# The first MLP product of the last token group by seven products of quarters, in matmuls of 128 columns

## The chip, the cores and the metric

The kernel runs on one core of a Trainium2 chip. A time is the device time of one execution in microseconds (us); lower is better. The kernel before takes 908.61 us, the median of three runs (908.17 to 909.64).

## The reference

Windowed causal attention over 8 batches, 8 heads, 576 positions and head size 64, with a linear bias, then an MLP on its output, all in float32:

```python
scores = scale * np.matmul(q, k.transpose(0, 1, 3, 2))
scores = np.where(mask, scores + bias[None], -1000000000.0)   # mask: 0 <= i - j < 128
attn = np.exp(scores - np.max(scores, axis=-1, keepdims=True))
attn = attn / (np.sum(attn, axis=-1, keepdims=True) + 1e-09)
x = np.matmul(attn, v).transpose(0, 2, 1, 3).reshape(B * S, H * D)     # 4608 x 512
h = x @ w_in                                                           # 512 x 2048
g = h * (1.0 / (1.0 + np.exp(-h)))
return g @ w_out                                                       # 2048 x 512
```

## The kernel before, in words

The 4608 tokens are worked in nine groups of 512 (group 0 to 8). A group's MLP has 16 steps, numbered through all groups (step 128 is the first of group 8, step 143 the last of all). A step makes one tile of 128 hidden features: its first product (`gemm1`) goes to a PSUM bank named `h`, of which there are two; `act1` (tanh, ScalarE), `act2` (multiply, VectorE), `act3` (the high half in f16, ScalarE) and `act4` (the low half, VectorE) make the activation; its second product (`gemm2`) adds into the banks of the output. Float32 precision comes from splitting every operand into a high and a low f16 half and multiplying three of the four pairs, so each product of 128 rows is three matmuls. The attention of the tokens to come is worked beside the MLP of the groups before.

Groups 7 and 8 (`FAST`) make the second product by Strassen's scheme in Winograd's form: seven products of quarters in place of eight, M1 to M7. For that a step is not one feature tile over 512 tokens, but two feature tiles (`j` and `j + 8`) over 256 tokens (`t` is 0 or 1): `gemm1_fast` fills one `h` bank with 2 x 12 matmuls of 256 columns, `act_sums` makes three sums of quarters of the activation, and `gemm2_fast` has 21 matmuls of 256 columns in two halves. The sums of `w_out` that the seven products need are made in advance by GpSimd (`SUM_WORK`), at positions 240 to 374, from late in group 3 to group 5. At the end of each eight steps `join_products` puts the output together from four banks.

The order of all work is written out by hand: a counter `pos` goes up by one for each half of a product, and `plan` holds for each position what else is issued there (`put`, `later`, `ahead`); each engine works its instructions in the order of issue. `LAG` says how many steps the second product stands behind the first in the last two groups: two before. `TAGS` constants name which finished buffer a new tile takes over.

Of the kernel before, what the change touches and what calls it, by code (L numbers as in the profile page):

```python
# [6 lines left out]
F32 = mybir.dt.float32  # L7
# [10 lines left out]
P = 128  # L18
# [12 lines left out]
TG = 512  # L31
# [36 lines left out]
Q16 = ("w1_2", "w1_3")  # L68
K16 = ("w1_4", "w1_5", "w1_6")
CUT = 2.0**-20  # L70
NB = 2
FAST = (NG - 2, NG - 1)
HALF_F = NF // 2
LAG = 2
SUMS, SUMS_STEP = 240, 18
OUT_TAGS = {3: ("w1_14", "w1_9"), 4: ("w1_13", "w1_14"), 6: ("w1_0", "w1_1")}
# [35 lines left out]
def tile_window_attention_then_silu_mlp(ctx, tc, qk, v, w_in, w_out, distance, out):  # L112
# [228 lines left out]
    def in_scale(b):  # L341

        if b == 0:
            wsc["in"] = pool.tile([P, NB], F32, tag="win", bufs=1, name="win")
            wsc["inv"] = pool.tile([P, NB], F32, tag="winv", bufs=1, name="winv")
            gsc["t", IN16] = pool.tile([P, NB], F32, tag="tsc", bufs=2, name=f"tsc{IN16}")
        n, inv = NF // NB, wsc["inv"][:, b : b + 1]
        scale_of(vred["w", 0]["m"][:, n * b : n * b + n], f"in{b}", 0, wsc["in"][:, b : b + 1], inv)
# [360 lines left out]
    def sum_lo(j, k):  # L709
# [4 lines left out]
        out16 = wsum[1, j]  # L714
        nc.gpsimd.tensor_sub(out16[:, 1], wsum["r"][:, 0, : DM // 2], out16[:, 0])

    def gemm1_fast(n, half):
# [53 lines left out]

    def act1(n):
        if n // NF in FAST:
            gact[n] = gt = pool.tile([P, 2 * TG], F32, tag="big", name=f"gt{n}")
# [64 lines left out]
    def gemm2_fast(n, half):  # L839
        g, (t, j) = n // NF, divmod(n % NF, HALF_F)  # L840
        last = LAST - 1 if n // HALF_F == LAST // HALF_F else n - j + HALF_F - 1
        if n == LAST:
            gemm2_last(half)
            return
        gh, gl, _ = gact.pop(n) if half else gact[n]
        products = (M5, M2, M1, M3) if half == 0 else (M4, M7, M6)
        for a, parts in ((gh, (0, 1)), (gl, (0,))):
            for k in products:
                b, side = PLACE[k]
                if j == 0 and side == 0 and a is gh:  # L850
                    ops[b] = psum.tile([P, DM], F32, tag=("axaz" if t else "wxyz")[b], bufs=2 if t and b % 2 == 0 else 1, name=f"m{g}_{t}_{b}")
# [52 lines left out]
    def join_products(g, t, half):  # L904

        scale = gsc[g][:, 2:3]
        if half == 0:
            st["out"] = [pool.tile([P, 2, DM // 2], F32, tag="q", bufs=2, name=f"of{g}_{t}_{k}") for k in range(2)]
# [229 lines left out]
    for j in range(HALF_F):  # L1138
        n = SUMS + SUMS_STEP * j
        for k, work in enumerate(SUM_WORK):  # L1140
            for fn, part in work:
                put(n + k, fn, j, part)
    put(STATS + 2 * NF + 6, out_scale)
    put(STATS + 2 * NF + 7, cut_scale)
    for which in range(2):
# [67 lines left out]
    with tc.manual_schedule():  # L1213
# [40 lines left out]
        for g in range(NG):  # L1254
# [3 lines left out]
            for f in range(NF):  # L1258
                n = g * NF + f
                waiting.append(n)  # L1260
                left = LAG if g in FAST else 1
                if f == NF - 1 and (g not in FAST or g == NG - 1):
                    left = 0
                seq += [("g1", n, 0), ("g1", n, 1)]
                while len(waiting) > left:
                    k = waiting.pop(0)
                    seq += [("g2", k, 0), ("g2", k, 1)]
            for k, n, half in seq:
                begin()
# [55 lines left out]
```

## Time and profile before

| what | value |
|---|---|
| runs of the kernel before | 908.17, 909.64, 908.61 us |
| the profiled execution's own time | 907.86 us |
| its span, first to last instruction | 905.7 us |
| TensorE matmuls busy | 896.4 us, 99% of the span |
| VectorE, ScalarE, GpSimd busy | 704.1, 584.0, 180.3 us |
| first products of groups 7 and 8 (L724) | 768 matmuls, 88.7 us |
| granted TensorE clock | 1.00 |

The page counts a matmul as busy until its modelled end, so the pace of TensorE is read from the starts of instructions in the timeline, not from their lengths. The last two groups run from about 743 us to the end; there the DMA engines and GpSimd have next to nothing to do.

### The profile page before, as it was taken

How to read it: one execution, taken by the hardware profiler on the slowest of the kernel's cores; microseconds unless marked ns; L12 is line 12 of the kernel's file. 1: busy time of each engine (PE TensorE's matmuls, PEld its weight loads, DVE VectorE, ACT ScalarE, POOL GpSimd, SP SyncE). 2: the span in 40 equal slices, each digit the busy share in tenths (PEclk: the TensorE clock that was granted, in tenths of full speed). 3: DMA queues.
4: the chain of work that ended last, by engine and by line, in shares of the span. 5: the costliest groups of instructions: out<-in, count | busy, mean ns of one | idle time of the engine just before them, and what ended most of it. 6: DMA issues, size and time to landing. Idle time of an engine off the chain costs nothing.

```text
span 905.7 us, 19202 instructions
## 1 busy us (share of the span) xinstructions
PE 896.4 (99%) x7369; PEld 591.5 (65%) x7369; DVE 704.1 (78%) x1755; ACT 584.0 (64%) x1200; POOL 180.3 (20%) x191
## 2 busy tenths in 40 slices
PE   9999999999999999999999999999999999999998
PEld 7877776888855555454445554455555558888887
DVE  6998998688978877677887787878776667667675
ACT  7789986776579855887666656657565554433342
POOL 2356662000000000012354332742000000000000
PEclk9999999999999999999999999999999999999999
DMA  9979724334489644994454536442753333000000
GB/s 323 398 180 268 233 58 129 71 94 94 105 218 232 179 94 120 241 229 120 88 147 106 106 80 144 99 99 59 158 123 95 69 77 77 12 13 24 1 25 24
DMA packets 198475, 113.58 MB, mean 125 GB/s; under 512 B 166256, under 2 KB 168432, under 8 KB 198384
## 3 DMA queue, kind: packets, MB, share of 16 engines
q1 hardware_dynamic: 197952, 111.97, 48.5%
q8 instruction: 58, 0.95, 0.5%
q10 hardware_dynamic: 432, 0.39, 0.1%
q14 instruction: 33, 0.27, 0.1%
HBM read 62.52 MB, written 9.44 MB: 79 GB/s over the span
## 4 chain that ended last, share of the span: by engine, by line
PE 84%; DVE 2%; ACT 1%; DMA 1%; issue 1%; DVEq 0%; ACTq 0%
PE o L946 29%; PE h L752 27%; PE h L724 9%; PE m L853 8%; PE av L582 4%; PE sp L477 3%; PE sp L484 2%; PE h L757 1%; DMA hl<-hr 1%; DVE gt L785 0%; DVE gl L829 0%; DVE v L458 0%; ACT wr L989 0%; ACT t L518 0%; ACT gh L815 0%
## 5 line engine op out<-in xcount | busy, mean ns | idle before, releaser
L946 PE MATMUL o<-w,gh 128*128 128x512 f16 (+1 forms) x896 | 273.6, 387 | 0.5 <-ACT gh L811 0.5
L752 PE MATMUL h<-xt,w 128*128 128x512 f16 (+1 forms) x1344 | 269.5, 349 | 0.0
L752 PEld LDWEIGHTS <-w 128*128 128x128 f16 x1344 | 126.4, 98 | 112.5 <-issue 3.3
L785 DVE SCALAR_TENSOR_TENSOR gt<-gt,h 128x512 f32<-128x512 f32 x144 | 98.5, 684 | 101.2 <-ACT gt L781 100.5
L781 ACT ACTIVATE gt<-h,tsc 128x512 f32<-128x512 f32 x128 | 87.4, 683 | 136.6 <-PE h L752 108.8
L946 PE MATMUL o<-w,gl 128*128 128x512 f16 (+1 forms) x448 | 172.1, 384 | 0.4 <-DVE gl L829 0.3
L518 ACT ACTIVATE t<-t,mx 128x256 f32<-128x256 f32 (+1 forms) x288 | 127.4, 488 | 42.8 <-DVE mx L508 41.4
L532 DVE SCALAR_TENSOR_TENSOR hr<-t,hr 128x512 f16<-128x512 f32 (+1 forms) x128 | 98.2, 772 | 16.8 <-ACT hr L527 16.2
L452 POOL TENSOR_SCALAR v<-rv,vsc 128x512 f16<-128x512 f32 x30 | 24.6, 820 | 419.6 <-DMA rv<-v 287.7
L946 PEld LDWEIGHTS <-gh 128*128 128x128 f16 x640 | 59.2, 98 | 66.1
L724 PE MATMUL h<-xt,w 128*128 128x256 f16 x768 | 88.7, 273 | 0.0
L815 ACT ACTIVATE gh<-gt,wcut 128x512 f16<-128x512 f32 x80 | 57.5, 719 | 36.9 <-DVE gt L785 36.2
L724 PEld LDWEIGHTS <-w 128*128 128x128 f16 x768 | 75.1, 98 | 8.9
L527 ACT ACTIVATE hr<-t 128x512 f16<-128x512 f32 (+1 forms) x128 | 74.3, 598 | 1.4 <-DMA hl<-hr 1.4
L829 DVE SCALAR_TENSOR_TENSOR gl<-gt,wcut,gh 128x512 f16<-128x512 f32 x80 | 63.9, 799 | 12.2 <-ACT gh L815 11.4
L582 PEld LDWEIGHTS <-hl 128*128 128x128 f16 x1464 | 51.9, 98 | 16.6 <-issue 5.6
L508 DVE CUSTOM_DVE_ANT_0 t<-sp,tab,vsc 128x256 f32<-128x256 f32 (+1 forms) x144 | 58.5, 461 | 0.1
L946 PEld LDWEIGHTS <-gl 128*128 128x128 f16 x320 | 31.3, 98 | 39.6 <-DVE gl L829 2.5
L582 PE MATMUL av<-v,hl 128*128 128x65 f16 (+1 forms) x1464 | 55.1, 193 | 1.7 <-DVE v L458 0.7
L946 PEld LDWEIGHTS o<-w,gh 128*128 128x128 f32 x256 | 45.7, 188 | 10.4 <-issue 1.0
L508 DVE CUSTOM_DVE_ANT_0 t<-sp,tab 128x256 f32<-128x256 f32 (+1 forms) x144 | 50.1, 402 | 1.2 <-PE sp L484 1.0
L160 POOL TENSOR_TENSOR w<-wm,w 128x512 fp32r<-128x512 f32 x32 | 44.6, 1393 | 2.6
(190 smaller groups left out, 1324.4 us busy)
## 6 DMA issues: line engine op xcount, KB each, us to landing
qs<-qk SPq DMA_DIRECT2D x18, 512.0 KB, 4.9
r<-qk SPq DMA_DIRECT2D x18, 512.0 KB, 4.6
wr<-w_in SPq DMA_DIRECT2D x16, 512.0 KB, 6.6
wr<-w_out SPq DMA_DIRECT2D x16, 512.0 KB, 6.4
rv<-v SPq DMA_DIRECT2D x30, 256.0 KB, 3.3
out<-ot SPq DMA_DIRECT2D x28, 256.0 KB, 2.9
vm<-v SPq DMA_DIRECT2D x27, 256.0 KB, 5.0
q<-qk SPq DMA_DIRECT2D x18, 256.0 KB, 3.7
```

What stands on the lines that cost most here:

```text
L508: nc.vector.tensor_tensor_reduce(out=st[p]["t"][u][:, h, 2 * P - n :], in0=st[p]["sp"][h][:, u, o].rearrange("p o c -> p (o c)"), in1=tab[ ...
L518: nc.scalar.activation(x, x, AF.Exp, bias=st[p]["mx"][:, 2 * u + h : 2 * u + h + 1], scale=-1.0)
L527: nc.scalar.activation(split_of(p, u, hr)[:, 0], t[:, :, 2 * P - n :], AF.Copy, scale=PSCALE)
L532: nc.vector.scalar_tensor_tensor(out=hr[:, 1], in0=t[:, :, 2 * P - n :], scalar=PSCALE, in1=hr[:, 0], op0=ALU.mult, op1=ALU.subtract)
L582: nc.tensor.matmul(av[:, 2 * u + h, : rhs.shape[-1]], lhs, rhs, start=(n == 0), stop=(n == len(seq) - 1), skip_group_check=True,)
L724: nc.tensor.matmul(out, w[:, wp, cc], xt[g, "g"][:, 2 * t : 2 * t + 2, xp * NCC + cc], start=half == 0 and i == 0, stop=i == len(seq) - 1, ...
L752: nc.tensor.matmul(o, w[:, wp, cc], x, start=start and k == 0, stop=stop, skip_group_check=True)
L781: nc.scalar.activation(gt, hps[n], AF.Tanh, scale=scale)
L785: nc.vector.scalar_tensor_tensor(out=gt, in0=gt, scalar=1.0, in1=hps[n], op0=ALU.add, op1=ALU.mult)
L829: nc.vector.scalar_tensor_tensor(out=gl, in0=gt, scalar=cut_of(n), in1=f32(gh) if n // NF < OUT16 else gh, op0=ALU.mult, op1=ALU.subtract)
L853: nc.tensor.matmul(product(k), a[:, k], sum_part(k, j, part), start=j == 0 and side == 0 and a is gh and part == 0, stop=n == last and a i ...
L946: nc.tensor.matmul(ops[ti], a[:, t], w, start=(f == 0 and i == 0), stop=(f == NF - 1 and i == len(seq) - 1), skip_group_check=True,)
```

## The change

Four things are changed together.

The first product of group 8 is made by seven products of quarters too (`gemm1_seven`). A step's feature tiles `j` and `j + 8` and its two token tiles make a 2 x 2 arrangement of quarters C11, C12, C21, C22, each of 128 x 128; the contraction is cut into two halves. C21 and C22 lie in an `h` bank, C11 and C12 in a second bank (`hb`, from the banks that held outputs of the second product). The seven products have six matmuls of 128 columns each. Three products go to more than one quarter: ScalarE copies them out of PSUM (`SNAP`, line L843: four copies of 128 columns a step) before the next product is added to the same quarter, and VectorE adds them to the other quarters at the end (`join_seven`, L852, twice a step). The step is cut into three pieces of 12, 18 and 12 matmuls, and the two halves of an older step's second product stand between them.

The sums of `w_in` that this needs are made by GpSimd (`in_float`, `in_make`, `in_lo`) with conversions on ScalarE (`in_hi`), at positions 391 to 496; the sums of x by VectorE (`x_float`, `x_make`, `x_part`) at 450 to 487, with four DMA transposes (`x_turn`). Buffers are moved for it: f16 halves of q and k are packed into three tiles, outputs into one.

In group 8 the three sums of the activation (`act_sums`) go from VectorE to GpSimd, and the second products stand three steps behind in group 7 (`LAG` 3) and four in group 8. Both token halves of group 8 use the same four output banks.

```diff
-LAG = 2
+LAG = 3
+IN_SUMS = (391, 405, 418, 431, 453, 464, 475, 486)
+X_SUMS = (450, 453, 456, 459, 462, 465, 468, 472, 471, 476, 474, 478, 479, 487, 481, 489)
+    def in_float(j, k):
+        w = w16[0, j + k * HALF_F]
+        nc.gpsimd.tensor_add(piece["r"][k].rearrange("p (c f) -> p c f", c=NCC), w[:, 0], w[:, 1])
+    SEQ = (("11", "11", C22), ("S1", "T1", C12)), (
+        ("S2", "T2", C22), ("12", "21", C11), ("S4", "22", C12)), (("S3", "T3", C22), ("22", "T4", C21))
+    SNAP = (("11", C22, C11), ("S1", C12, C22)), (("S2", C22, C12),), (("S3", C22, C21),)
+    def gemm1_seven(n, which):
+        if which == 0:
+            hps[n] = [ps_of("h", f"h{n}"), ps_of("wy"[n % 2], f"hb{n}")]
...
+        for w, x, to in SEQ[which]:
+            terms = [(a, b, cc) for cc in range(2) for a, b in ((0, 0), (0, 1), (1, 0))]
+            for i, (a, b, cc) in enumerate(terms):
+                nc.tensor.matmul(
+                    h[to], w_of(j, w, a, cc), x_of(g, t, x, b, cc),
...
+        for w, of, at4 in SNAP[which]:
+            nc.scalar.copy(hsum[n][:, at4], h[of])
+        if which:
+            join_seven(n, 2 - which)
...
-        engine, a = nc.vector, gact[n]
+        engine, a = nc.gpsimd if n // NF == SEVEN else nc.vector, gact[n]
...
-                left = LAG if g in FAST else 1
+                left = LAG + (g == SEVEN) if g in FAST else 1
...
+                if g == SEVEN and then:
+                    seq += [first[0], then[0], first[1], then[1], first[2], *then[2:]]
...
+                            ahead((11, 8, 6)[max(0, n - LAST + 3)], act4, n)
+                            ahead((9, 7, 6)[max(0, n - LAST + 3)], act3, n)
+                            ahead(3, act2, n)
+                            ahead(2, act1, n)
```

ScalarE where group 8 begins, before: `gt126` to `gt128` are the tanh and the high halves of steps 126 to 128 (L781 is `act1`, L805 `act3`).

```order
L781 ACTIVATE gt126_11095<-h126_11070,tsc7_9998 128x512
L805 ACTIVATE gh126_11113<-gt126_11095,wcut_3103 128x640
L805 ACTIVATE gh126_11113<-gt126_11095,wcut_3103 128x256
L781 ACTIVATE gt127_11153<-h127_11128,tsc7_9998 128x512
L805 ACTIVATE gt127_11159<-gt127_11153,wcut_3103 128x640
L805 ACTIVATE gt127_11159<-gt127_11153,wcut_3103 128x256
L781 ACTIVATE gt128_11211<-h128_11186,tsc8_11065 128x512
```

The same place after (L930 is `act1`, L954 `act3`, L843 the copies, `hs128` what they fill):

```order
L930 ACTIVATE gt126_11169<-h126_11140,tsc7_10014 128x512
L843 COPY hs128_11252<-h128_11250 128x128
L843 COPY hs128_11252<-hb128_11251 128x128
L930 ACTIVATE gt127_11267<-h127_11204,tsc7_10014 128x512
L843 COPY hs128_11252<-h128_11250 128x128 x2
L843 COPY hs129_11310<-h129_11308 128x128
L843 COPY hs129_11310<-hb129_11309 128x128
L954 ACTIVATE gh126_11325<-gt126_11169,wcut_3103 128x640
L954 ACTIVATE gh126_11325<-gt126_11169,wcut_3103 128x256
L930 ACTIVATE gmore_11329<-hj128_11288,tsc8_11176 128x512
L843 COPY hs129_11310<-h129_11308 128x128
```

Between step 126's tanh and its high half there now stand seven instructions, among them the copies of step 128, and the copy of step 129's second piece stands behind the tanh of step 128.

VectorE there, before (L785 is `act2`, L795 to L797 the sums, L822 `act4`):

```order
L822 SCALAR_TENSOR_TENSOR gl126_11114<-gt126_11095,wcut_3103,gh126_11113 128x640
L822 SCALAR_TENSOR_TENSOR gl126_11114<-gt126_11095,wcut_3103,gh126_11113 128x256
L785 SCALAR_TENSOR_TENSOR gt127_11153<-gt127_11153,h127_11128 128x512
L795 TENSOR_TENSOR gt127_11153<-gt127_11153 128x256
L796 TENSOR_TENSOR gt127_11153<-gt127_11153 128x256
L797 TENSOR_TENSOR gt127_11153<-gt127_11153 128x128
L822 SCALAR_TENSOR_TENSOR io127_11160<-gt127_11153,wcut_3103,gt127_11159 128x640
L822 SCALAR_TENSOR_TENSOR io127_11160<-gt127_11153,wcut_3103,gt127_11159 128x256
L785 SCALAR_TENSOR_TENSOR gt128_11211<-gt128_11211,h128_11186 128x512
```

The same place after (L852 is the joining of step 128 or 129, L934 `act2`, L944 to L946 the sums, L971 `act4`):

```order
L852 SCALAR_TENSOR_TENSOR hj128_11288<-hb128_11251,hs128_11252 128x256
L934 SCALAR_TENSOR_TENSOR gt127_11267<-gt127_11267,h127_11204 128x512
L944 TENSOR_TENSOR gt127_11267<-gt127_11267 128x256
L945 TENSOR_TENSOR gt127_11267<-gt127_11267 128x256
L946 TENSOR_TENSOR gt127_11267<-gt127_11267 128x128
L852 SCALAR_TENSOR_TENSOR hj128_11288<-h128_11250,hs128_11252 128x256
L934 SCALAR_TENSOR_TENSOR gmore_11329<-gmore_11329,hj128_11288 128x512
L971 SCALAR_TENSOR_TENSOR gl126_11326<-gt126_11169,wcut_3103,gh126_11325 128x640
L971 SCALAR_TENSOR_TENSOR gl126_11326<-gt126_11169,wcut_3103,gh126_11325 128x256
L852 SCALAR_TENSOR_TENSOR hj129_11368<-hb129_11309,hs129_11310 128x256
L971 SCALAR_TENSOR_TENSOR io127_11371<-gt127_11267,wcut_3103,gt127_11370 128x640
```

Step 127's multiply now stands behind the first joining of step 128, and step 126's and 127's low halves behind the multiply of step 128.

ScalarE at the end, before (step 143 is the last, `once8_1` belongs to the output):

```order
L805 ACTIVATE gt141_12019<-gt141_12001,wcut_3103 128x640
L805 ACTIVATE gt141_12019<-gt141_12001,wcut_3103 128x256
L781 ACTIVATE gt142_12059<-h142_12034,tsc8_11065 128x512
L805 ACTIVATE gh142_12077<-gt142_12059,wcut_3103 128x640
L805 ACTIVATE gh142_12077<-gt142_12059,wcut_3103 128x256
L781 ACTIVATE gt143_12117<-h143_12092,tsc8_11065 128x512
L805 ACTIVATE gt143_12120<-gt143_12117,wcut_3103 128x512
```

The same place after:

```order
L843 COPY hs143_12534<-h143_12532 128x128
L843 COPY hs143_12534<-hb143_12533 128x128
L954 ACTIVATE gt141_12549<-gt141_12464,wcut_3103 128x640
L954 ACTIVATE gt141_12549<-gt141_12464,wcut_3103 128x256
L930 ACTIVATE gmore_11329<-hj142_12501,tsc8_11176 128x512
L843 COPY hs143_12534<-h143_12532 128x128 x2
L930 ACTIVATE gt143_12616<-hj143_12591,tsc8_11176 128x512
L954 ACTIVATE gt143_12619<-gt143_12616,wcut_3103 128x512
L954 ACTIVATE gh142_12623<-gmore_11329,wcut_3103 128x640
L954 ACTIVATE gh142_12623<-gmore_11329,wcut_3103 128x256
```

The high half of step 142 stood ahead of the tanh of step 143, and now stands behind the tanh and the high half of step 143.

## Rows read from the trace of the kernel before

**Rows 1.** Windows: busy time (and instructions) of each engine, granted clock, DMA share, GB/s.

```profile
490.00:540.00 50.00, 50.00 (x425) 25.46 (x425) 38.75 (x100) 33.28 (x65) 21.43 (x22) 1.00 0.40 86
540.00:590.00 50.00, 49.38 (x384) 24.14 (x379) 41.25 (x94) 31.18 (x64) 25.46 (x24) 1.00 0.58 122
690.00:743.00 53.00, 53.00 (x450) 26.91 (x448) 36.69 (x97) 29.43 (x56) 1.40 (x2) 1.00 0.29 69
770.00:823.00 53.00, 53.00 (x488) 47.49 (x487) 35.95 (x75) 21.34 (x34) 0.00 (x0) 1.00 0.03 11
865.00:905.70 40.70, 36.86 (x338) 32.79 (x336) 26.18 (x53) 14.28 (x22) 0.00 (x0) 0.99 0.08 27
```

**Rows 2.** Timeline near the end, TensorE: start, length (us), line, operation, count.

```profile
882.05 2.78 PE L724 MATMUL h<-xt,w 128*128 128x256 f16 x24
...
884.67 0.60 PE L853 MATMUL m<-w,gt 128*128 128x256 f16 x4
...
886.96 2.78 PE L724 MATMUL h<-xt,w 128*128 128x256 f16 x24
```

**Rows 3.** Timeline of TensorE before the last two groups: the short matmuls and what follows them.

```profile
723.50 0.84 PE L477 MATMUL sp<-h,h 64*128 64x128 f16 x24
724.27 1.47 PE L752 MATMUL h<-xt,w 128*128 128x512 f16 x6
...
729.46 0.88 PE L582 MATMUL av<-v,hl 128*128 128x65 f16 x24
730.18 1.46 PE L752 MATMUL h<-xt,w 128*128 128x512 f16 x6
```

**Rows 4.** Timeline near the end: the activation chain of one step on ScalarE and VectorE.

```profile
884.93 0.69 ACT L781 ACTIVATE gt<-h,tsc 128x512 f32<-128x512 f32 x1 [1.12 <-PE h L724]
...
885.65 0.69 DVE L785 SCALAR_TENSOR_TENSOR gt<-gt,h 128x512 f32<-128x512 f32 x1 [0.93 <-ACT gt L781]
...
887.49 1.23 ACT L805 ACTIVATE gt<-gt,wcut 128x640 f16<-128x640 f32 x2 [1.88 <-DVE gt L797]
```

**Rows 5.** Groups by line and form, ScalarE, whole span: busy, mean ns | idle before.

```profile
L805 ACT ACTIVATE gh<-gt,wcut 128x640 f16<-128x640 f32 x16 | 13.3, 828 | 33.5 <-DVE gt L797 33.5
...
L1229 ACT ACTIVATE tab<-rel 128x128 bf16<-128x128 f32 x8 | 1.7, 295 | 1.5 <-DMA rel<-distance 1.5
```

**Rows 6.** Groups by line and form, VectorE, 800 to 850 us.

```profile
L785 DVE SCALAR_TENSOR_TENSOR gt<-gt,h 128x512 f32<-128x512 f32 x10 | 6.9, 686 | 6.7 <-ACT gt L781 6.7
...
L822 DVE SCALAR_TENSOR_TENSOR gl<-gt,wcut,gh 128x640 f16<-128x640 f32 x5 | 4.4, 884 | 4.5 <-ACT gh L805 4.5
L795 DVE TENSOR_TENSOR gt<-gt 128x256 f32<-128x256 f32 x10 | 4.2, 424 | 0.3
...
L822 DVE SCALAR_TENSOR_TENSOR gl<-gt,wcut,gh 128x256 f16<-128x256 f32 x5 | 2.4, 478 | 0.0
...
L896 DVE SCALAR_TENSOR_TENSOR of<-m,gsc,of 128x256 f32<-128x256 f32 x2 | 0.9, 474 | 0.0
L888 DVE SCALAR_TENSOR_TENSOR of<-m,gsc,of 128x512 f32<-128x512 f32 x1 | 0.8, 751 | 0.1
```

**Rows 7.** Groups by line and form, GpSimd, 400 to 906 us.

```profile
L674 POOL TENSOR_TENSOR wr<-w 128x512 f32<-128x512 f16 x16 | 21.0, 1331 | 0.0
L712 POOL TENSOR_TENSOR ws<-wq,ws 128x512 f16<-128x512 f32 x16 | 20.7, 1301 | 53.8 <-ACT ws L703 53.8
...
L687 POOL TENSOR_TENSOR wq<-wr 128x256 f32<-128x256 f32 x8 | 7.8, 972 | 0.0
```

**Rows 8.** Groups by line and form, VectorE, 480 to 590 us.

```profile
L829 DVE SCALAR_TENSOR_TENSOR gl<-gt,wcut,gh 128x512 f16<-128x512 f32 x19 | 17.0, 897 | 2.5 <-ACT gh L815 2.4
```

**Rows 9.** Groups by line and form, VectorE, 690 to 740 us.

```profile
L829 DVE SCALAR_TENSOR_TENSOR gl<-gt,wcut,gh 128x512 f16<-128x512 f32 x9 | 6.7, 747 | 1.3 <-ACT gh L815 1.2
```

**Rows 10.** Timeline at the very end: last matmul, last stores issued.

```profile
901.59 0.27 PE L876 MATMUL last<-w,io 128*128 128x256 f16 x1
...
902.00 1.11 SPq L902 DMA_DIRECT2D out<-of  x2
```

More of the change, by code (lines that the diff above doesn't have):

```diff
@@ L715, in sum_lo, with in_pieces @@
         nc.gpsimd.tensor_sub(out16[:, 1], wsum["r"][:, 0, : DM // 2], out16[:, 0])
+    win, piece = {}, {}
+    def in_pieces(j):
+        if IN_SUMS[j] < (NG - 2) * SLICE * NF:
+            both = [pool.tile([P, 2, DM], F32, tag="big", name=f"wb{j}_{k}") for k in range(2)]
+            t = [b[:, s] for b in both for s in range(2)]
+        else:
+            if "own" not in piece:
+                piece["own"] = pool.tile([P, DM], F32, tag="k", bufs=KSLOTS, name="wown")
+            t = [pool.tile([P, DM], F32, tag="t", bufs=3, name=f"wb{j}_{k}") for k in range(3)] + [piece["own"]]
+        piece["r"], piece["q"] = t[:2], [a.rearrange("p (s c) -> p s c", s=2) for a in t[2:]]
+        if j in IN_TAGS:
+            w = pool.tile([P, 2, 4, DM // 2], F16, tag=IN_TAGS[j], bufs=1, name=f"wx{j}")
+            win[j] = [w[:, part] for part in range(2)]
+        elif j < HALF_F - 1:
+            tag, bufs = ("q", 2) if j < 4 else ("x", 4)
+            w = [pool.tile([P, 4, DM // 2], F16, tag=tag, bufs=bufs, name=f"wx{j}_{part}") for part in range(2)]
+            win[j] = [a[:] for a in w]
+        else:
+            flat = [a.rearrange("p s h d -> p (s h d)")[:, : 2 * DM] for a in (v1, v2)]
+            win[j] = [a.rearrange("p (s c) -> p s c", s=4) for a in flat]
@@ new lines, in in_float, with in_make @@
+    def in_float(j, k):
+        if k == 0:
+            in_pieces(j)
+        w = w16[0, j + k * HALF_F]
+        nc.gpsimd.tensor_add(piece["r"][k].rearrange("p (c f) -> p c f", c=NCC), w[:, 0], w[:, 1])
+    def in_make(j, k):
+        (a11, a12), (a21, a22) = ([r[:, h * DM // 2 : (h + 1) * DM // 2] for h in range(2)] for r in piece["r"])
+        one, two = piece["q"]
+        if k == 0:
+            nc.gpsimd.tensor_add(one[:, 0], a21, a22)
+            nc.gpsimd.tensor_sub(one[:, 1], one[:, 0], a11)
+        else:
+            nc.gpsimd.tensor_sub(two[:, 0], a11, a21)
+            nc.gpsimd.tensor_sub(two[:, 1], a12, one[:, 1])
@@ new lines, in in_hi, with in_lo, x_float @@
+    def in_hi(j, k):
+        nc.scalar.copy(win[j][0][:, 2 * k : 2 * k + 2], piece["q"][k])
+    def in_lo(j, k):
+        hi, lo = (a[:, 2 * k : 2 * k + 2] for a in win[j])
+        nc.gpsimd.tensor_sub(lo, piece["q"][k], hi)
+    xsum, xf = {}, []
+    def x_float(i):
+        if not xf:
+            xf.extend(pool.tile([P, 2, 2, DM // 2], F32, tag=tag, bufs=1, name=f"x_{tag}") for tag in X_TAGS)
+        t, k = divmod(i % GT, 2)
+        nc.vector.tensor_add(xf[k][:, t].rearrange("p q c -> p (q c)"), xt[i][:, 0], xt[i][:, 1])
@@ new lines, in x_make, with x_part @@
+    def x_make(k):
+        (b11, b21), (b12, b22) = ([a[:, :, q] for q in range(2)] for a in xf)
+        out, a, b = ((b11, b12, b11), (b12, b22, b12), (b22, b22, b11), (b21, b21, b22))[k]
+        minus(nc.vector, out, a, b)
+    def x_part(k, part):
+        flat = xf[k].rearrange("p t q c -> p (t q c)")
+        xsum["r", k, part] = hr = pool.tile([P, 8 * P], F16, tag="hr", bufs=2, name=f"xr{k}_{part}")
+        if part == 0:
+            nc.scalar.copy(hr, flat)
+        else:
+            minus(nc.vector, hr, flat, xsum["r", k, 0])
@@ new lines, in x_turn @@
+    def x_turn(k, part):
+        xsum[k, part] = hl = pool.tile([P, 8, P], F16, tag="hl", bufs=4, name=f"xq{k}_{part}")
+        nc.sync.dma_start_transpose(hl, xsum["r", k, part])
+    X_WORK = (
+        (x_float, NTILE - 4), (x_float, NTILE - 3), (x_float, NTILE - 2), (x_float, NTILE - 1),
+        (x_make, 0), (x_make, 1), (x_make, 2), (x_part, 1, 0), (x_make, 3), (x_part, 1, 1), (x_turn, 1, 0), (x_turn, 1, 1),
+        (x_part, 0, 0), (x_part, 0, 1), (x_turn, 0, 0), (x_turn, 0, 1),
+    )
@@ new lines, in tile_window_attention_then_silu_mlp, with w_of @@
+    IN_WORK = (
+        [(in_float, 0)], [(in_float, 1)], [(in_make, 0)], [], [(in_make, 1)], [], [(in_hi, 0)], [(in_lo, 0)],
+        [(in_hi, 1)], [(in_lo, 1)],
+    )
+    C21, C22, C11, C12 = range(4)
+    SEQ = (("11", "11", C22), ("S1", "T1", C12)), (
+        ("S2", "T2", C22), ("12", "21", C11), ("S4", "22", C12)), (("S3", "T3", C22), ("22", "T4", C21))
+    SNAP = (("11", C22, C11), ("S1", C12, C22)), (("S2", C22, C12),), (("S3", C22, C21),)
+    hsum = {}
+    def w_of(j, name, part, cc):
+        if name[0] == "S":
+            k = int(name[1]) - 1
+            return win[j][part][:, k, cc * P : (cc + 1) * P]
+        row, col = (int(c) - 1 for c in name)
+        return w16[0, j + HALF_F * row][:, part, 2 * col + cc]
@@ new lines, in join_seven @@
+    def join_seven(n, side):
+        if side:
+            hsum[n, "h"] = pool.tile([P, TG], F32, tag="t", bufs=3, name=f"hj{n}")
+        cols = slice(side * TG // 2, (side + 1) * TG // 2)
+        nc.vector.scalar_tensor_tensor(
+            out=hsum[n, "h"][:, cols], in0=hps[n][side][:, : TG // 2], scalar=1.0,
+            in1=hsum[n].rearrange("p k c -> p (k c)")[:, cols], op0=ALU.mult, op1=ALU.add,
+        )
+        if not side:
+            hps[n] = hsum.pop((n, "h"))
+            del hsum[n]
@@ L773, in act1 @@
         if n // NF in FAST:
-            gact[n] = gt = pool.tile([P, 2 * TG], F32, tag="big", name=f"gt{n}")
+            if n // NF == SEVEN and n % 2 == 0:
+                if "more" not in gact:
+                    gact["more"] = pool.tile([P, 2, 2 * TG], F32, tag="xh" if SEVEN % 2 == 0 else "xl", bufs=1, name="gmore")
+                gt = gact["more"][:, n // 2 % 2]
+            else:
+                gt = pool.tile([P, 2 * TG], F32, tag="big", name=f"gt{n}")
+            gact[n] = gt
             gt = gt[:, :TG]
@@ L845, in gemm2_fast @@
         gh, gl, _ = gact.pop(n) if half else gact[n]
-        products = (M5, M2, M1, M3) if half == 0 else (M4, M7, M6)
+        products, first = (M5, M2, M1, M3, M4, M7, M6), 4
+        if j == 0 and g == SEVEN:
+            first = 3
+        elif j == 0 and t:
+            products = (M3, M4, M5, M2, M1, M7, M6)
+        products = products[first:] if half else products[:first]
         for a, parts in ((gh, (0, 1)), (gl, (0,))):
@@ L907, in join_products @@
         if half == 0:
-            st["out"] = [pool.tile([P, 2, DM // 2], F32, tag="q", bufs=2, name=f"of{g}_{t}_{k}") for k in range(2)]
+            both = pool.tile([P, 2, 2, DM // 2], F32, tag="w1_6", bufs=1, name=f"of{g}_{t}")
+            st["out"] = [both[:, k] for k in range(2)]
             st["once"] = once = pool.tile([P, 2, DM // 2], F32, tag="rv", bufs=2, name=f"once{g}_{t}")
@@ L1142, in tile_window_attention_then_silu_mlp @@
                 put(n + k, fn, j, part)
+    for j in range(HALF_F):
+        for k, work in enumerate(IN_WORK):
+            for fn, part in work:
+                put(IN_SUMS[j] + k, fn, j, part)
+    for k, (fn, *a) in enumerate(X_WORK):
+        put(X_SUMS[k], fn, *a)
     put(STATS + 2 * NF + 6, out_scale)
```

75 lines of the change are left out of this document (55 added, 20 removed).

## The prediction

> **What bounds the kernel now.** I read the windows first, then the timeline of the last two groups, then the groups of each engine. The windows show TensorE busy in the whole of every stretch from 690 us to near the end, at a granted clock of 1.00 [rows 1]; that alone proves little, since a matmul counts as busy to its modelled end, so I check the pace: 24 matmuls of 256 columns take 884.67 - 882.05 = 2.62 us, and the 21 of a second product 886.96 - 884.67 = 2.29 us [rows 2], 109 ns each in both. TensorE never waits there; a step is 4.91 us. ScalarE and VectorE have room: from 770 to 823 us they are busy 21.3 and 36.0 of 53 us. GpSimd does nothing then [rows 1]. After the last matmul at 901.59 us only the last additions and stores follow, to 905.7 [rows 10]; the change leaves them alone. So time can be won only by less work on TensorE, and lost only where TensorE is made to wait.
>
> **What the first product saves.** 24 x 16 = 384 matmuls of 256 columns go, at 109.2 ns: 41.9 us. 42 x 16 = 672 of 128 columns come. The trace has none with a full 128 x 128 weight load and 128 columns, so I bound it. Half of the 256-column matmul, 54.6 ns, is the low end. The 24 matmuls of mostly 65 columns, each with its own weight load, take 730.18 - 729.46 = 0.72 us, 30 ns each, so a weight load hides even there [rows 3]. The 24 score matmuls run in pairs, 12 x 128 columns in 0.77 us, 64 ns a pair, which is the high end [rows 3]. At the granted full clock of 2.4 GHz, 256 columns are 106.7 ns, so 2.5 ns are fixed; 128 columns then take 53.3 + 2.5 = 55.8 ns. I take that, since the 65-column row bears it out (27.1 + 2.5 = 29.6). A step's 42 take 2.35 us, 16 steps 37.5 us: 4.4 us saved (5.2 at the low end, a loss of 1.1 at the high one). The step becomes 2.35 + 2.29 = 4.64 us. The second products are the same number, only later and in another order.
>
> The Trainium skill ("TensorE: Matmul & The Clock Gate", "Back-to-back issue gap") states about 81 ns per matmul for a sustained stream of weight loads and matmuls of 128 columns. By it the new product would take 672 x 81 = 54.4 us, an estimate from that page, and the change would lose 12.5 us. The 30 ns of the 65-column stream speak against it here.
>
> **What TensorE waits for in group 8.** New on its path is that ScalarE must have copied a quarter out of PSUM before the next product is added to it. A result reaches ScalarE 0.26 us after the next matmul's start (884.93 against 884.67) [rows 2, 4]. The copy of 128 columns has no row; the nearest is a 128 x 128 conversion at 0.295 us [rows 5], and the end above is the 0.69 of 512 columns [rows 4]. I take 0.30. In a steady step it is hidden: the first piece ends at 0.67 us into the step, its copies at 1.2; the half of the second product between takes 1.3 us, so the next piece starts at 2.0. ScalarE has 4 x 0.30 + 0.69 + 1.23 = 3.1 us of work a step, VectorE 2 x 0.47 (joining, by the 474 ns of an addition of PSUM to SBUF) + 0.69 + 0.88 + 0.48 = 3.0 us, GpSimd three sums [rows 4, 6], all under 4.64. But not every step is steady:
>
> - *Start of group 8.* Step 128 has no second product between its pieces. Counted from its first matmul: its first product is complete at 0.33 + 0.26, copied at 0.89; the second piece would start at 0.67 and starts 0.25 late. ScalarE then makes the second copy (1.22) and the tanh of step 127 (1.91), and only then the copy for the third piece (2.2), 0.3 late. Step 129 needs the `h` bank of step 127, which VectorE frees with that step's multiply; that stands behind the first joining of step 128 (result at 2.16, done at 2.63), done 3.32, where TensorE is ready at 2.87: 0.5 late. VectorE now has step 127's sums (1.1), a joining, a multiply, then two low halves of 1.36 to do in a row; the joining of step 129 ends at about 11.3, its tanh at 12.0, the copy behind it in ScalarE's queue at 12.3, and the third piece of step 130 was due at 11.9: 0.45. Together 1.5 us.
> - *Where outputs are put together* (steps 127 and 135, worked off in steps 131 and 139): VectorE gets 2 x 0.47 + 0.75 + 2 x 0.47 + 0.75 = 3.4 us more in one step, the last joining of that step ends 3.2 us into the next, the tanh 0.7 later, the copy another 0.3; the third piece is due at 4.0: 0.35 late, twice 0.7.
> - *The end.* The last first product ends 4.6 us into step 143. Then VectorE joins (to 6.6), tanh 7.4, multiply 8.1, high half of step 143 8.9, and only behind it the high half of step 142, first part at 9.7; its second product is due after those of steps 140 and 141, at 4.6 + 2 x 2.29 = 9.2: 0.55, and 0.15 more for its low half. 0.7 us.
>
> In all 2.9 us. Below, if copies end sooner or I have a queue wrong at half of the places, 1.5; above, if GpSimd slows VectorE there, 4.5.
>
> **What the preparation costs in groups 6 and 7.** For each of eight pairs of tiles GpSimd has 2 additions of 512 columns (1.33), 4 of 256 (0.97) and 2 subtractions of 512 (1.30), 9.1 us [rows 7]; 73 us in all, in about 160. It delays VectorE: the low half of 512 columns takes 897 ns where GpSimd works and 747 where not [rows 8, 9]. What that does to TensorE: with GpSimd busy 25.5 us of 50, TensorE was busy 49.38; with 21.4, all 50; with 1.4, all 53 [rows 1]. So between 0 and 0.6 us for 25 us of such work. The half in group 6, 36 us, costs 0 to 0.9; I take 0.4, the middle of two rows that disagree. In group 7 the additions for x are 8 operations of 512 columns and 2 of 1024 on VectorE, about 8 x 0.7 + 2 x 1.5 = 8.6 us by the rows for 512 [rows 6], in a stretch where it is idle 17 of 53 us [rows 1]; second products one step later give the chain 4.9 us more. I take 0, with 3 us as the upper end if the slowing of VectorE by a fifth (0.2 x 54 = 11 us) and the 8.6 use up its idle time. The ScalarE conversions (16 of 512 and 2 of 1024 columns, some 12 us) lie in its idle 32 of 53. The four transposes are issued some 16 positions ahead of their use. Packed and moved buffers cost nothing: ScalarE waits before each conversion of q and k for the same load as before.
>
> **The sum.** -4.4 + 2.9 + 0.4 = -1.1 us. The profiled execution took 907.86 us, 906.8 with the change; it lies 0.75 under the median of 908.61, so the median to expect is 907.5.
>
> **Rivals.**
>
> *The copies and queues cost far less.* If the waits are 1 us and groups 6 and 7 nothing, the gain is 3.4 to 4.2 and the time 904.4 to 905.2. For it: all engines have room in a steady step. Against it: ScalarE works its queue in order, and the tanh that waits for VectorE stands ahead of copies that TensorE needs.
>
> *VectorE becomes the bound of group 8.* GpSimd has two sums of 256 and one of 128 columns a step, about 2 x 0.97 + 0.5 = 2.4 us. If every VectorE operation stood still for that, a step would need 3.0 + 2.4 = 5.4 us, 0.8 over TensorE's 4.64, and over 13 steps 10 us are lost: 908.6 - 4.4 + 10 + 0.7 = 915. It decides where VectorE is slowed by over half (4.64 / 3.0). The rows show a fifth, with GpSimd at work about half of the time, so some 40% while both work: near, but under it.
>
> *Groups 6 and 7 take it back.* VectorE's idle time in group 7 is used up, steps 113 to 125 wait for `h` banks: 3 + 0.9 us in place of 0.4, and 4.5 for the waits of group 8: -4.4 + 8.4 = +4.0, 912.6; with either alone 909 to 911. It decides where the waits pass 4.4 us.
>
> *A weight load does not hide behind 128 columns.* By the rows' pair of 64 ns the first product loses 1.1 us, and the time is 908.6 + 1.1 + 3.3 = 913. The 30 ns row all but excludes it. The skill's rule named above is of this kind.
>
> **Chances.** A measurement tells a change of 0.2%, 1.8 us, from none. My forecast, a gain or loss smaller than that, 0.42; the first rival and what lies between it and the forecast, 0.40; slower 0.18: VectorE as the bound 0.06, groups 6 and 7 0.10, weight loads 0.02. The range goes from 904.6, where the waits nearly vanish, to 910.2, where waits of 6 us outweigh the saving; beyond lie about 0.1 on either side.
>
> **What would show it.** In the new profile: 42 matmuls of 128 columns a step at 55 to 57 ns, steps 133 to 138 at 4.6 us without idle TensorE; idle TensorE ended by ScalarE (L843) in steps 128 to 131, 139 and 140, and by ScalarE (L954) or VectorE (L971) before the second product of step 142, 0.3 to 0.7 us each; group 7 no longer than before. I am wrong if the matmuls take over 60 ns, if steady steps wait, or if VectorE is busy throughout in group 7 or 8.

## The result and the profile after

The time went up: 915.43 us (914.34 to 916.00) against 908.57 us (908.17 to 909.64) of the kernel before in the same rounds, a ratio of 1.0072 with a 95% interval of 1.0055 to 1.0090. The forecast was 907.5 us, 904.6 to 910.2. The profiled execution has a span of 913.7 us, 8.0 over that of before.

The two traces differ in three places after the first quarter of the program (to the 2000th matmul, at some 256 us, the profiled executions differ by up to 2.2 us, whatever the kernel; here it is 0.6). Group 6 became 1.6 us longer. From the first matmul of group 7's MLP to the first of group 8's it was 743.45 to 818.18 us and is now 745.73 to 827.28, 6.8 us more, though one second product (2.29 us) less lies in it: 9.1 us lost. From there to the last matmul it was 83.7 us and is now 82.5 with one second product more: 3.5 us gained. The windows show the place, beside [rows 1] (columns as there):

```profile
690.00:743.00 53.00, 52.73 (x444) 26.58 (x443) 42.69 (x99) 31.17 (x60) 25.36 (x22) 1.00 0.30 71
743.00:770.00 27.00, 27.00 (x262) 23.14 (x259) 22.20 (x43) 13.61 (x25) 9.70 (x9) 1.00 0.42 98
770.00:823.00 53.00, 46.82 (x404) 40.19 (x403) 46.73 (x68) 23.42 (x38) 22.82 (x23) 0.94 0.12 31
823.00:865.00 42.00, 41.51 (x549) 38.92 (x548) 29.59 (x59) 24.19 (x61) 15.14 (x21) 1.00 0.04 14
```

From 770 to 823 us TensorE is idle for 6.2 us where it was never idle, and the mean granted clock is 0.94; VectorE went from 36.0 to 46.7 us, GpSimd from 0 to 22.8. What TensorE waited for, over groups 7 and 8 to 831 us (engine, line, what it waited for: total us, times, longest):

```profile
PE m L1007 <- DVE of L1067: 3.2, 1, 3.2
PE m L1007 <- ACT once L1065: 1.7, 1, 1.7
PE m L1007 <- DVE gl L971: 1.0, 2, 0.7
PE h L838 <- DVE gt L934: 0.5, 1, 0.5
PE h L867 <- DVE gt L934: 0.3, 1, 0.3
```

From 831 us to the last matmul the same view names no wait, and for the kernel before it names none from 640 us on. In lines of after, 1007 is the second product (853 before), 867 the 24 matmuls of 256 columns (724), 838 the new ones of 128, 934 the multiply (785), 944 to 946 its sums (795 to 797), 971 the low half (822), 1065 to 1072 the putting together of the output, 754 to 771 GpSimd's new sums. The largest wait in the timeline, all engines but the weight loads (start, length, engine, line):

```profile
798.07 0.60 PE L1007 MATMUL m<-ws,gh 128*128 128x256 f16 x4
798.53 0.60 ACT L767 CAST wx<-wown 128x512 f16<-128x512 f32 x1
799.03 0.68 ACT L930 ACTIVATE gt<-h,tsc 128x512 f32<-128x512 f32 x1
799.62 0.67 ACT L1065 ACTIVATE once<-m,gsc 128x512 f32<-128x512 f32 x1
799.75 0.69 DVE L934 SCALAR_TENSOR_TENSOR gt<-gt,h 128x512 f32<-128x512 f32 x1 [1.20 <-ACT gt L930]
800.32 2.44 POOL L754 TENSOR_TENSOR wb<-w 128x512 f32<-128x512 f16 x2
800.34 0.60 PE L1007 MATMUL m<-w,gh 128*128 128x256 f16 x4 [1.67 <-ACT once L1065]
800.47 1.28 DVE L944 TENSOR_TENSOR gt<-gt 128x256 f32<-128x256 f32 x1
801.67 1.37 DVE L945 TENSOR_TENSOR gt<-gt 128x256 f32<-128x256 f32 x1
...
803.07 0.69 DVE L946 TENSOR_TENSOR gt<-gt 128x128 f32<-128x128 f32 x1
803.69 0.86 DVE L1067 SCALAR_TENSOR_TENSOR of<-m,gsc,once 128x256 f32<-128x256 f32 x2
...
804.61 1.01 PE L1007 MATMUL m<-ws,gh 128*128 128x256 f16 x4 [3.23 <-DVE of L1067]
...
806.48 3.93 PE L867 MATMUL h<-xt,w 128*128 128x256 f16 x24
810.25 0.60 PE L1007 MATMUL m<-w,gt 128*128 128x256 f16 x4
```

Step 119's products are being put together here. ScalarE's `once`, which frees a PSUM bank, stands behind a conversion for GpSimd's sums and a tanh; VectorE's `of`, which frees the next, stands behind three sums. Those take 1.28, 1.37 and 0.69 us, while GpSimd's additions of lines 754 and 760 run; alone they take 0.42, 0.42 and 0.29 (e.g. at 790.5 us). During the wait of 3.2 us the granted clock of TensorE falls to 0.50, and it comes back at about 808.8 us, among the 24 matmuls from 806.48 (granted clock: the last number but two of each row):

```profile
804.61:806.48 1.87, 1.87 (x10) 1.31 (x9) 1.87 (x2) 0.42 (x2) 1.76 (x2) 0.50 0.00 0
806.48:810.25 3.77, 3.77 (x26) 2.94 (x25) 3.67 (x7) 0.69 (x1) 0.00 (x0) 0.69 0.31 102
```

The nine matmuls from 804.61 take 1.87 us in place of 0.98, and the 24 from 806.48 take 3.77 instead of the 2.62 of [rows 2]. Idle TensorE 6.2 us, matmuls at the lower clock 2.0, and some 0.8 that the modelled ends hide (five waits): the 9.1.

In group 8 the change does what was computed. TensorE in two steady steps (start, length; the spans between starts are what counts):

```profile
866.95 0.50 PE L838 MATMUL h<-xq,wx 128*128 128x128 f16 x6
867.29 0.50 PE L838 MATMUL h<-xq,w 128*128 128x128 f16 x6
867.62 0.50 PE L838 MATMUL h<-xt,w 128*128 128x128 f16 x6
867.96 0.50 PE L838 MATMUL hb<-xq,wx 128*128 128x128 f16 x6
868.29 0.60 PE L1007 MATMUL m<-w,gt 128*128 128x256 f16 x4
...
871.59 0.50 PE L838 MATMUL h<-xq,wx 128*128 128x128 f16 x6
...
876.23 0.50 PE L838 MATMUL h<-xq,wx 128*128 128x128 f16 x6
```

Six matmuls of 128 columns take 0.333 us, 56 ns each, and a step 4.64 us against 4.91.

### The profile page after: what moved, and what is told of

Same layout as the page of the kernel before. It is cut to its first block, busy times and chain, and to the rows that moved or that the text cites. A ratio compares the mean times of both kernels' runs of the same rounds, so it can differ in the third digit from the quotient of the medians.

```text
span 913.7 us, 20003 instructions
## 1 busy us (share of the span) xinstructions
PE 897.1 (98%) x7657; PEld 593.0 (65%) x7657; DVE 730.8 (80%) x1752; ACT 607.2 (66%) x1282; POOL 282.1 (31%) x300
## 4 chain that ended last, share of the span: by engine, by line
PE 74%; DVE 10%; ACT 3%; issue 1%; DMA 1%; DVEq 0%; ACTq 0%; SPq 0%
PE o L1101 27%; PE h L895 25%; PE m L1007 6%; PE av L590 4%; PE sp L485 3%; PE h L838 2%; PE sp L492 2%; PE hb L838 2%; PE h L867 2%; DVE gt L934 1%; PE h L900 1%; ACT gt L930 1%; DVE gt L944 1%; DVE t L516 1%; DVE gt L945 1%
## 5 line engine op out<-in xcount | busy, mean ns | idle before, releaser
L895 PEld LDWEIGHTS <-w 128*128 128x128 f16 x1344 | 126.4, 98 | 112.5 <-issue 3.3
L934 DVE SCALAR_TENSOR_TENSOR gt<-gt,h 128x512 f32<-128x512 f32 x128 | 87.4, 683 | 81.6 <-ACT gt L930 80.8
L930 ACT ACTIVATE gt<-h,tsc 128x512 f32<-128x512 f32 x112 | 76.4, 683 | 109.9 <-PE h L895 99.3
L978 DVE SCALAR_TENSOR_TENSOR gl<-gt,wcut,gh 128x512 f16<-128x512 f32 x80 | 66.5, 831 | 12.0 <-ACT gh L964 11.4
L167 DVE SCALAR_TENSOR_TENSOR x<-xs,x 128x256 f16<-128x256 f32 x64 | 34.8, 544 | 13.7 <-ACT x L629 13.5
L867 PE MATMUL h<-xt,w 128*128 128x256 f16 x384 | 45.4, 277 | 0.3 <-DVE gt L934 0.3
```

What stands on the lines that cost most here:

```text
L867: nc.tensor.matmul(out, w[:, wp, cc], xt[g, "g"][:, 2 * t : 2 * t + 2, xp * NCC + cc], start=half == 0 and i == 0, stop=i == len(seq) - 1, ...
L895: nc.tensor.matmul(o, w[:, wp, cc], x, start=start and k == 0, stop=stop, skip_group_check=True)
L934: nc.vector.scalar_tensor_tensor(out=gt, in0=gt, scalar=1.0, in1=hps[n], op0=ALU.add, op1=ALU.mult)
L978: nc.vector.scalar_tensor_tensor(out=gl, in0=gt, scalar=cut_of(n), in1=f32(gh) if n // NF < OUT16 else gh, op0=ALU.mult, op1=ALU.subtract)
```

## The experiments

All ratios are to the kernel before, run on the same chip beside each kernel, with 95% intervals. Theory A: a VectorE operation with two operands in SBUF stands still while a GpSimd operation runs, and GpSimd's sums of pairs 4 to 7, which fall into group 7, cost the 9 us. B: VectorE is filled by its own additions for x. C: the conversions `act3` and `act4`, two positions later in group 7, make the queues tight. D: only pair 7, which falls on the putting together of step 119. E: the chain through ScalarE's queue, and not the memory port.

**e1_no_w_sums_g7: group 7 without GpSimd's sums.**

```
-    for j in range(HALF_F):        # IN_WORK
+    for j in range(4):
-            return win[j][part][...]
+            return win[j % 4][part][...]
```

> The changed kernel (915.4 us) with the sums of w_in for pairs 4 to 7 left out on GpSimd and ScalarE; the products use the sums of pairs 0 to 3 twice, so a part of the sums isn't computed. Theory A (in group 7 a VectorE operation stands still while a GpSimd operation runs, and the 36 us of GpSimd's work there cost the 9 us): group 7 without idle TensorE, 906 to 907.5 us. Theory B (VectorE's own additions for x use up its idle time): 913 to 915. Theory C (the high and low halves of group 7 are issued two positions later, which ties a step's tanh to the low half of two steps before): 913 to 915. Theory D (only the pair 7, which falls on the place where outputs are put together, hurts): 908 to 910, since pair 7 is gone here too.

906.34 us, ratio 0.9976 (0.9965 to 0.9987): 9 us below after. The window that lost 6.2 us loses 0.5 here, the wait at step 129, which is already group 8:

```profile
770.00:823.00 53.00, 52.53 (x507) 47.11 (x505) 38.72 (x81) 22.23 (x38) 0.00 (x0) 1.00 0.15 31
```

A window of fixed length holds less of the work in after, which is late by then. From the first matmul of group 7's MLP to the first of group 8's, after and then e1:

```profile
745.73:827.28 81.55, 75.37 (x683) 65.84 (x682) 71.03 (x118) 34.58 (x57) 31.91 (x31) 0.96 0.22 53
745.90:818.34 72.44, 72.44 (x682) 65.00 (x681) 56.56 (x118) 30.71 (x49) 0.00 (x0) 1.00 0.26 59
```

The whole 9.1 us of group 7 are gone. VectorE's same 118 operations, the x additions among them, are busy 56.6 us, not 71.0: 14.5 us of after were standing still. GpSimd's sums in group 7, or ScalarE's conversions that go with them, are the cause; by which way is not yet told.

**e2_no_x_sums: without VectorE's additions for x.**

```
-    for k, (fn, *a) in enumerate(X_WORK):
-        put(X_SUMS[k], fn, *a)
-            return xsum[k, part][...]
+            return xt[g, "g"][...]
```

> The changed kernel with the sums of x left out (12 VectorE operations, two ScalarE conversions, four transposes); the products read x itself in their place, so that part isn't computed. A: 1 to 3 us are won, 912 to 914.5, and TensorE still stands idle between 787 and 806 us. B: 907 to 909. C: 914 to 915.5.

913.49 us, 1.0053 (1.0037 to 1.0069): 2 us less than after, and the wait of 3.2 us stays. B is a small part.

**e3_late2: `late` as before.**

```
- ... else 4 if g in FAST and n % NF > 1 else 2
+ ... else 2
```

> The changed kernel with the high and low halves of group 7's activations issued two positions after the first product, as in the kernel before, in place of four. C: the tanh no longer waits for low halves, 907 to 910. A: the same VectorE work at other places, 913 to 916. B: 914 to 916.

916.60 us, 1.0089 (1.0071 to 1.0107), 0.6 us above the range that A gave. C falls: earlier conversions make it no better.

**e4_shift7: pair 7 later.**

```
-IN_SUMS = (391, 405, 418, 431, 453, 464, 475, 486)
+IN_SUMS = (391, 405, 418, 431, 453, 464, 475, 494)   # and x_part, x_turn up to 4 positions later
```

> The changed kernel with pair 7's sums 8 positions later (494 in place of 486) and the last low half of x and its transpose 4 positions later, so that neither falls on the putting together of step 119's outputs. D: the two waits of 1.7 and 3.2 us and the slower clock behind them go, 908.5 to 910.5. A: half of it goes, since VectorE is late there from pairs 5 and 6 already, 911 to 914. B and C: 914 to 916.

915.77 us, 1.0078 (1.0062 to 1.0094), the same waits to 0.1 us, and not the half that A expected to go. Neither D nor that part of A was tested: GpSimd's queue held nothing else, so pair 7's additions started right behind pair 6's last low half as before (801.83 us). A later place in the order of issue does not hold back an engine that has nothing to do.

**e6_memsets: GpSimd works in group 7, but reads nothing.**

```
         w = w16[0, j + k * HALF_F]
+        if j > 3:
+            for _ in range(2):
+                nc.gpsimd.memset(piece["r"][k], 0.0)
+            return
```

and likewise, two fills for each operation, in `in_make` and `in_lo`.

> For pairs 4 to 7, the ones prepared in group 7, each GpSimd operation that reads two tiles is replaced by two fills of the same tile, which read nothing; ScalarE's conversions, the order and all dependencies stay, the sums are not computed. Theory A (a VectorE operation with two operands in SBUF stands still while GpSimd reads SBUF): the stall at the putting together of step 119 goes, time 906 to 908.5 us. Rival E (the stall is made by the chain of dependencies and by ScalarE's queue behind GpSimd, not by the port): time stays 912 to 915.5 us.

906.06 us, 0.9976 (0.9967 to 0.9985). E falls for group 7: dependencies, ScalarE's conversions and the order are those of after, and no wait of group 7 is left. First after, then this kernel, VectorE and GpSimd in the timeline:

```profile
782.82 1.16 POOL L771 TENSOR_TENSOR wx<-wown,wx 128x512 f16<-128x512 f32 x1 [4.12 <-ACT wx L767]
782.99 1.26 DVE L944 TENSOR_TENSOR gt<-gt 128x256 f32<-128x256 f32 x1
783.93 2.63 POOL L754 TENSOR_TENSOR wb<-w 128x512 f32<-128x512 f16 x2
784.17 1.37 DVE L945 TENSOR_TENSOR gt<-gt 128x256 f32<-128x256 f32 x1
785.58 1.12 DVE L946 TENSOR_TENSOR gt<-gt 128x128 f32<-128x128 f32 x1
786.63 2.27 DVE L971 SCALAR_TENSOR_TENSOR gl<-gt,wcut,gh 128x640 f16<-128x640 f32 x2
```

```profile
791.24 2.15 POOL L782 MEMSET v<- 128x512 f16 x4
791.93 0.43 DVE L957 TENSOR_TENSOR gt<-gt 128x256 f32<-128x256 f32 x1
792.28 0.42 DVE L958 TENSOR_TENSOR gt<-gt 128x256 f32<-128x256 f32 x1
792.73 0.29 DVE L959 TENSOR_TENSOR gt<-gt 128x128 f32<-128x128 f32 x1
```

In after each of the three sums ends 0.15 to 0.28 us after a GpSimd operation ends, however long that one ran, and the next sum lasts until behind GpSimd's next: they take turns, operation by operation. Beside fills the same sums run at full pace: of 128 x 256, 8 alone with a median of 426 ns and 8 overlapping a fill with 425. (The fills are shorter, 11.1 us of GpSimd in the window instead of 22.8; the sums that overlap them show that it isn't this alone.) The Trainium skill says so in "SBUF — State Buffer", "Who interferes with whom": VectorE and GpSimd share a port pair under an exclusive lock, and a VectorE instruction with two SBUF inputs contends with a GpSimd instruction that reads SBUF, not with one that only writes. The traces agree in both halves.

**e7_no_sums_no_x:** the edits of e1 and e2 together.

> Pairs 4 to 7 use the sums of pairs 0 to 3, and the sums of x are left out as well. Theory A: little under the 906.3 us of the run without pairs 4 to 7 alone, 904.5 to 906 us, since the additions of x find VectorE free once GpSimd is still. If x costs 2 us by itself: 904.3 us.

906.67 us, 0.9979 (0.9969 to 0.9989): not under the run without pairs 4 to 7 alone, as A had it, but the same. The x additions cost nothing when GpSimd is still; their 2 us exist only on top of its work.

**e5_lag3_only:** the kernel before with `LAG = 3`.

> The kernel before with its second products one step later (LAG 3) and nothing else of the change. All theories: 908 to 909.5 us, no change, since a step in between has no idle TensorE either way. If the longer chain at the end or fuller buffers matter: over 910 us.

908.58 us, 1.0003 (0.9994 to 1.0013). The later second products cost nothing.

**v1_late67: pairs 6 and 7 made to wait for x's tiles.**

```
+        elif j >= 6:     # pieces: xf, the two float tiles of x
+            t = [a.rearrange("p t q c -> p (t q c)")[:, k * DM : (k + 1) * DM] for a in xf for k in range(2)]
-IN_SUMS = (..., 475, 486)
+IN_SUMS = (..., 490, 524)
```

> Nothing is left out. Pairs 6 and 7 take the two tiles of x as their pieces, so that GpSimd can't begin pair 6 before x is done with (position 487) and pair 7 before the 132nd step. Theory A: GpSimd does nothing while step 119 is put together, the stalls of 3.2 and 1.7 us there go, time 906.5 to 909.5 us. If the cost moves with GpSimd's work into group 8: 911 to 914 us. If that work doesn't matter: 915 us.

913.50 us, 1.0053 (1.0036 to 1.0069). Of the two large waits at step 119 one is gone and the other shrank to 0.7, but 3.7 us of new ones came in group 8:

```profile
PE h L840 <- ACT hs L845: 3.7, 2, 1.9
PE m L1009 <- DVE of L1069: 0.7, 1, 0.7
```

The first line's two waits are for copies of a quarter. The one that ends at 823.7 us is behind a tanh that waited for a low half; shortly before, at 814 to 816.5 us, two sums had taken 1.26 and 1.37 us beside GpSimd. The one that ends at 849.5 us is behind a conversion that waited 3.2 us for GpSimd's additions: here ScalarE's queue passes GpSimd's lateness on to TensorE, which is the way of E. Moving the work moved the cost.

**v3_vec67: pairs 6 and 7 on VectorE.** The pieces as in v1, and for pairs 6 and 7

```
-        nc.gpsimd.tensor_add(...)      # all sums of in_float, in_make, in_lo
+        (nc.vector if j >= 6 else nc.gpsimd).tensor_add(...)
-IN_SUMS = (..., 475, 486)
+IN_SUMS = (..., 493, 515)
```

> Nothing is left out. The additions of pairs 6 and 7 are made by VectorE (8 operations of 0.42 to 0.75 us each, 4.6 us a pair) instead of GpSimd (9.1 us a pair), pair 6 behind the putting together of step 119, pair 7 in the first steps of group 8. Theory A: VectorE pays 9 us of its own idle time instead of standing still, the stalls of 3.2 and 1.7 us go, 907 to 909.5 us. If VectorE is simply too full, with or without GpSimd: 911 to 914 us.

909.62 us, 1.0008 (1.0000 to 1.0017), just over A's range: the same additions cost 6 us less than in after, and 4 less than in v1, where GpSimd makes them at much the same late positions. They are cheaper by the engine that they would have blocked.

**v4_vec67_early:** v3, and pairs 0 to 3 three positions earlier (388, 402, 415, 428).

> As the kernel with pairs 6 and 7 on VectorE, and pairs 0 to 3 begin three positions (about 3.5 us) earlier, so that GpSimd's additions fall on other VectorE operations of group 6. Theory A: where they fall decides, the two waits for a low half there (0.5 and 0.43 us) go or move: 0.5 to 1 us below the other. If only their number counts: the same time.

908.07 us, 0.9993 (0.9984 to 1.0002). In group 6 the two waits for a low half (line 978 in after; 1.2 us together in v3's view of waits, as in after) are gone; 0.7 at the putting together of step 119 and 2 us at that of step 127, among pair 7's additions, remain.

**v2_six and v2_four: seven products for 6 or for 4 of the 8 pairs**, plain products of 256 columns and no sums for the others.

```
+                    few = n % HALF_F >= MANY
+                    if not few:
+                        gemm1_seven(n, half)
+                    elif half < 2:
+                        gemm1(n, half)
```

> Seven products only for the first 6 of the 8 pairs of tiles; steps with pairs 6 and 7 use the 24 products of 256 columns, so pairs 6 and 7 need no sums. 12 of 16 steps save 0.27 us: -3.3. Theory A: the stalls at step 119 shrink to about 1 us, since GpSimd is still after 785 us; group 6 costs 1 to 1.6 as before; 907.5 to 909.5 us. If GpSimd's work isn't the cause: 915 us + 1.1.

> Seven products only for the first 4 pairs, so GpSimd makes no sums in group 7; the sums of x stay. 8 steps save 0.27 us: -2.2; group 6 costs 1 us, group 7 nothing by theory A: 907 to 908.5 us. If the additions of x alone fill VectorE in group 7: 910 us or more.

908.64 us, 1.0001 (0.9992 to 1.0010), and 908.09 us, 0.9992 (0.9983 to 1.0002). Both as theory A had it.

**v5_pair7_sooner:** v4 with `IN_SUMS[7] = 508`. **v6_seven_pairs:** v4 with `MANY = 7`, pair 7 plain. **v7_four_early:** v2_four with pairs 0 to 3 as in v4.

> As v4_vec67_early, with pair 7's additions (VectorE) seven positions earlier, before step 127 is put together. If the place decides: the wait of 2.1 us in 837 to 840 us goes, 906 to 907 us. If VectorE is too full at the end of group 7 instead: the wait moves to 815 to 825 us, 908 to 910 us.

> As v4_vec67_early, but pair 7 needs no sums: its two steps use the 24 products of 256 columns. 0.55 us of TensorE's saving given up, the 2.1 us of waiting at the putting together of step 127 gone: 906.3 to 907 us, below before by 0.2%. If that wait isn't from pair 7's additions: 908.5 us.

> As v2_four, with pairs 0 to 3 begun three positions earlier and nothing else. If the place of the additions decides in group 6: its two waits (0.51 and 0.43 us) go, 907.1 us against 908.1. If not: 908.1 us.

In this order: 907.13 us, 0.9983 (0.9975 to 0.9992); 906.64 us, 0.9976 (0.9966 to 0.9986); 907.51 us, 0.9988 (0.9979 to 0.9997). v7 is 0.6 us under v2_four where 1.0 was expected, with intervals that overlap; its trace has neither of the two waits. v5's wait at 837 us went, one of 1.1 us came at 829.7, and the time is just over the range given for it. v6 is faster than the kernel before and than the changed one, with nothing left out. All that TensorE waits for in it from 648 us on:

```profile
PE m L1015 <- DVE of L1075: 0.7, 1, 0.7
PE h L846 <- DVE gt L942: 0.5, 1, 0.5
```

Its group 7 (columns as above) takes 0.9 us more than e1's, though VectorE has only 8.2 us left idle there:

```profile
743.99:817.31 73.32, 72.60 (x682) 65.00 (x681) 65.15 (x125) 33.89 (x55) 15.26 (x15) 1.00 0.24 59
```

## Why the prediction was wrong

**The saving was right.** 56 ns a matmul against 55.8, a step of 4.64 us, 4.4 us saved. The 81 ns of the Trainium skill ("TensorE: Matmul & The Clock Gate", "Back-to-back issue gap") was rightly not followed: 641 gaps between such matmuls, each with its own weight load, have a median of 56 ns.

**The waits of group 8 were taken too high:** 2.9 us, measured about 0.9 by the spans between starts (0.6 at step 129 for the `h` bank, where I had 0.5, and 0.3 around the copies in step 128). The other terms, the joinings in steps 131 and 139 and the end, have no wait at all. The copy is 0.27 us long, close to the 0.30, but what stands behind a copy and has nothing to wait for starts 0.16 us after its start:

```profile
896.32 0.27 ACT L843 COPY hs<-h 128x128 f32<-128x128 f32 x1 [0.40 <-PE hb L838]
896.48 0.27 ACT L843 COPY hs<-hb 128x128 f32<-128x128 f32 x1
...
896.64 1.24 ACT L954 ACTIVATE gt<-gt,wcut 128x640 f16<-128x640 f32 x2
```

I summed lengths where a queue overlaps them; at the end, for one, the last two joinings start 0.34 us apart and not 0.47. How much of the other terms this explains was not worked out. This error was on the good side.

**"In group 7 ... I take 0, with 3 us as the upper end" is the step that failed; measured 9.1 us.** The amount of slowing was too low even for the upper end: I wrote a fifth of 54 us, 11 us, and the 118 operations of group 7 stood still for 14.5 us. But above all it was wrong to set such a sum against the 17 of 53 us in which VectorE was idle. In after VectorE is still idle for 10.5 of group 7's 81.6 us, while TensorE waits; in v6 it is idle for 8.2 of 73.3 us, and group 7 costs 0.9 us. So it isn't the idle time left over that decides, but where the slowed operations fall. The mean of a fifth in [rows 8] could have shown it: of its 19 operations 14 take 740 to 752 ns, and five, all beside GpSimd, 1111 to 1639. In group 7 the sums of 128 x 256 that meet GpSimd last up to three times as long, and they come in bunches: in the step at 783 us the three sums and the low half take 5.9 us instead of 2.3, in the one at 800 us the three sums 3.3 instead of 1.1. A step is 4.91 us, and each result is wanted within a step or so. Idle time of other steps doesn't help, and what stands behind in the queue (the putting together of step 119, which frees PSUM) is late by the whole bunch.

**Group 6, "I take 0.4", cost 1.6 us** in the profiled execution, over the 0.9 of its bound; the traces of other runs with nearly the same order there (e1 to e7 but e5, v1, v3, v2) have 0.9 to 2.4. The rows that bounded it ([rows 1]) had means again. v4 and v7 have the same eight operations per pair three positions earlier and cost 0 and 0.4, without these waits: what was to be looked for was which VectorE operation with a result wanted at once, here line 978, falls beside which GpSimd operation.

**The rivals.** "Groups 6 and 7 take it back" had the right place, but 912.6 us at most. "VectorE becomes the bound of group 8" had the right mechanism, every VectorE operation standing still for GpSimd's, with 915 us; but it placed it in group 8, where GpSimd's sums mostly run while VectorE has nothing with two SBUF operands to do (12 of 35 low-half operations meet one, and none of the multiplies), and the 915 is a coincidence. What spoke against both in the prediction was the same mean. The second products later (LAG 3) cost 0, as said.

## What to carry to other kernels

Before work is given to an idle GpSimd, list the VectorE operations with two operands in SBUF that could run at the same time, and add to each the length of the GpSimd operation in its way; judge that step by step against when the result is wanted, not against VectorE's idle time over a long window. Work of that kind may be cheaper on VectorE itself (here 4.4 us for pair 6 in v3, instead of 8.7 a pair on GpSimd in after), and the last of a batch of such preparations may not be worth its saving: seven of eight pairs gave 906.6 us, eight gave 907.1 at best, with intervals that overlap. An engine that has nothing to do starts early whatever its place in the order; only a dependency holds it back.

## What the runs showed of the hardware

- The VectorE operations with one operand in PSUM are untouched by GpSimd here: the multiply of line 934 has a median of 687 ns alone and beside GpSimd in group 7, the joining of line 852 one of 424 in group 8. Those with both in SBUF take turns with it: 128 x 256 sums 0.42 us alone, a median of 1.26 and 1.37 us beside additions, 0.43 beside fills.
- Seven us of waits cost 9: in the longest, of 3.2 us, the granted clock of TensorE fell from 1.00 to 0.50 (from 2.4 to 1.2 GHz). Matmuls of 256 columns then started 213 ns apart, and only from 808.8 us on, among the 24 that began at 806.48, 109 ns again.
